# Softmax end in column halves, the last two chunks' logits by replicated weights, side products of the second MoE in batches, two more weight buffers

## The chip, the cores and the metric

One NeuronCore of a Trainium2 chip. Its engines run beside each other and meet by semaphores: PE (matrix products, into PSUM), PEld (the loading of the stationary operand for them), DVE (vector), ACT (activation functions, copies), POOL (general purpose) and SP, which here issues all the DMA transfers. The metric is the device time of one execution in microseconds (us); lower is better.

## The reference

Three layers follow each other on 1536 tokens of width 512:

```python
x = attention(q, k, v)              # clustered: a query sees the keys of its own cluster
h = x @ w_in                        # 1536 x 2048
g = (a0 + a1*h + a2*h*h + a3*h**3) / (1 + |b0|*|h| + |b1|*h*h + 1e-6)
x = g @ w_out                       # 1536 x 512, input of the second MoE
logits = x @ phi                    # 1536 x 32: 8 experts with 4 slots each
d = softmax(logits over the tokens) # axis 0
slot_input = (d.T @ x).reshape(8, 4, 512)
slot_out[e] = relu(slot_input[e] @ w1[e]) @ w2[e]     # 512 -> 1024 -> 512, 8 experts
c = softmax(logits over the slots)  # axis 1
out = c @ slot_out                  # 1536 x 512
```

## The kernel before, in words

The attention takes the first part of the span and isn't touched. What follows is written as if `w_out` came late: `logits` are made as `g @ (w_out @ phi)`, with `w_out @ phi` (the tile `wphi`) ready beforehand, and `d.T @ x` as `(d.T @ g) @ w_out`. So `g` is kept, `w_out` is applied to 32 slots and not to 1536 tokens, and the end of the kernel is a chain of small products.

*The unit loop.* The 1536 tokens are 3 blocks `t` of 512, the 2048 hidden columns 16 chunks `f` of 128; a unit n is one chunk of one block, 48 in all. `h_mm` makes h for a unit on PE (12 matrix products); `s1`, `s2`, `s3` make g from it on ACT, POOL and DVE (the last unit in two column halves); `s4`, four units later, turns g by four transposes (tile `gt`), copies it into the weight slots `gsl` on ACT, and every fourth unit adds four chunks to the logits: four products with 32 rows each (tile `l`), one in each quarter of the 128 rows, which run side by side. So row 32k+s of `l` holds slot s for the chunks of class k.

*The end of a block* (`block_end`): `e0` adds the four classes with the constant matrix `sum4` (tile `lsum`; every row then holds its slot's full logit, four times over) and takes the negative running maximum `nM` over the tokens; `e0b` turns the logits (`lt`) for the softmax over slots, and makes exp on ACT; `e2` turns exp (`dt`); `e3` makes `d.T @ g` (tile `dg`, 16 products of 512 columns in four quarters) and adds it to the running sum `U`. For blocks 0 and 1 this is spread over the next units. For block 2 it stands at the end, with nothing left to cover it.

*The chain behind it*: U is turned (`ut`, `uT`), multiplied by `w_out` (16 products, line 992), scaled by 1/sum (`sin`), turned and summed over the classes (line 999, `sT`), then by `w1` for experts 0 to 3 (line 1012, 32 products of 512 columns), relu, turned (line 1024) into the tile `HZ`; the same for experts 4 to 7; then the three softmaxes over slots are turned for the output (line 1036). Then `w2` (line 1083) in three column groups of 256, 128 and 128 columns, 64 products each; after each group `out_steps` sums the result over the row quarters (line 1047), splits it into a high and a low part (`SO4`, lines 1049 and 1051), multiplies by c (line 1058: six, three and three products) and copies the rows to the tile `ob`, from which SP writes 256 KB of output each (line 1069).

*Weights.* `w_out` (4 MB), `w1` (16 MB) and `w2` (16 MB) come as 36 loads of 1 MB in a fixed order (`queue`), the 16 of `w1` by halves of the contraction, 8 for experts 0 to 3 and then 8 for experts 4 to 7; those of `w2` are 8, 4 and 4 for the column groups. `freed` issues the next load when a buffer is given to it: one at every third unit while the list `waiting` has a buffer, then those freed at the end (the input's tiles, the unit loop's working tiles, the four `gsl` tiles after `dg`), then one for each weight tile that `used` says is read. There are 14 slots of 8 KB per partition (`NSLOT`): nine go to weights at first, five hold g. SP issues in program order, and a load that waits for its buffer holds up the ones behind it.

*Order.* PE's and SP's order is the program's; in the unit loop ACT's, DVE's and POOL's is set by a scheduler. `warm` puts in products whose result nobody reads.

Of the kernel before, what the change touches and what calls it, by code (L numbers as in the profile page):

```python
# [58 lines left out]
def tile_kernel(ctx, tc, qT, kT, v, cenT, cenP, consts, constsb, ab, w_in, w_out, phi, w1, w2, out, dbg=None):  # L59
# [665 lines left out]
    U = keep.tile([128, 512], F32, name="U")  # L725
    wphi = keep.tile([128, NF, NS], F32, name="wphi")
    POOL.tensor_scalar(wphi, wphi0, 1.0, 1.0, ALU.mult, ALU.mult)
    rctx.close()
    NSLOT = 14
# [99 lines left out]

    def s4(n):  # L830
# [3 lines left out]
        if k == 0:  # L834
            gsl[t, j] = sl_tile(F32, f"g{t}{j}")
        ps = psT.tile([128, 512], F32, tag="t", name="gt")
        for i in range(4):
            PE.transpose(ps[:, i * 128:(i + 1) * 128], g[:, i * 128:(i + 1) * 128], ident)  # L838
        ACT.copy(gsl[t, j][:, :, k * 128:(k + 1) * 128], ps.rearrange("p (i f) -> p i f", i=4))
        if k == 3:  # L840
            if j == 0:
                lps[t] = psL.tile([128, 512], F32, tag="l", name="l")
            for kk in range(4):
                PE.matmul(lps[t][32 * kk:32 * kk + 32, :], wphi[:, 4 * j + kk, :], gts.pop(n - 3 + kk),  # L844
                          start=(j == 0), stop=(j == 3))
            if j == 3:
                Ls[t] = keep.tile([128, 512], F32, tag="L", name="L")
                DVE.tensor_copy(Ls[t], lps.pop(t))


    def block_end(t):
# [13 lines left out]
        def e0b():  # L865
# [5 lines left out]
            if t == NB - 1:  # L871
                hold["dT"] = a_tile("dT")
# [25 lines left out]
        def e3():  # L898
# [11 lines left out]
            if t == NB - 1:  # L910
                freed(sl_tile, 4)

        return [e0, e0b, e2, e3, e1]

    def warm(k):

        for _ in range(k):
            ps = psH.tile([128, 512], F32, tag="h", name="warm")
            PE.matmul(ps[:, 0:256], ident, cst[:, 0:256], start=True, stop=True)
# [8 lines left out]
    for n in range(nunit + LAG):  # L928
# [6 lines left out]
        if 0 <= n - LAG:  # L935
            s4(n - LAG)
            if (n - LAG) % NF == NF - 1:
# [12 lines left out]
    manual = tc.manual_schedule(engines={mybir.EngineType.PE})  # L950
# [4 lines left out]
    sl2_p = ctx.enter_context(tc.tile_pool(name="sl2", bufs=4, reuse_waits="tile"))  # L955
    a_p = ctx.enter_context(tc.tile_pool(name="ap", bufs=3, reuse_waits="tile"))
    d_p = ctx.enter_context(tc.tile_pool(name="dp", bufs=1, reuse_waits="tile"))

    def sl2_tile(dt, name):
        return sl2_p.tile([128, 4, 512], dt, tag="sl2", name=name)  # L960
# [5 lines left out]
    for e in ends:  # L966
        e()
        warm(1)
    ps = psT.tile([128, 512], F32, tag="t", name="ut")
    for k in range(4):  # L970
        PE.transpose(ps[:, k * 128:(k + 1) * 128], U[:, k * 128:(k + 1) * 128], ident)
# [188 lines left out]
```

## Time and profile before

| | us |
|---|---|
| three runs | 548.85, 548.89, 549.78 |
| median | 548.89 |
| the profiled execution, its own time | 547.26 |
| its span, first to last instruction | 545.5 |
| PE busy in the span | 524.1 |

The span is cut by the profile into instructions of each engine. A row of the timeline or the chain gives a start, a duration and what ran; "issue" is time in which nothing that the profile shows was waited for.

### The profile page before, as it was taken

How to read it: one execution, taken by the hardware profiler on the slowest of the kernel's cores; microseconds unless marked ns; L12 is line 12 of the kernel's file. 1: busy time of each engine (PE TensorE's matmuls, PEld its weight loads, DVE VectorE, ACT ScalarE, POOL GpSimd, SP SyncE). 2: the span in 40 equal slices, each digit the busy share in tenths (PEclk: the TensorE clock that was granted, in tenths of full speed). 3: DMA queues.
4: the chain of work that ended last, by engine and by line, in shares of the span. 5: the costliest groups of instructions: out<-in, count | busy, mean ns of one | idle time of the engine just before them, and what ended most of it. 6: DMA issues, size and time to landing. Idle time of an engine off the chain costs nothing.

```text
span 545.5 us, 10069 instructions
## 1 busy us (share of the span) xinstructions
PE 524.1 (96%) x3518; PEld 342.3 (63%) x3521; DVE 414.0 (76%) x801; ACT 381.0 (70%) x693; POOL 274.5 (50%) x314
## 2 busy tenths in 40 slices
PE   8989999999999999999999999999999999988994
PEld 3555666566566666665666777777777767743463
DVE  6678889888798897988652799999799988941143
ACT  2777888869788788797874788878587868820111
POOL 3435767467655786567523655555455535601000
PEclk9999999999999999999999999999999999999999
DMA  8959869597767886667331566866567656479997
GB/s 231 281 141 255 240 206 268 185 256 192 247 192 233 252 247 191 211 198 195 126 101 59 192 245 225 295 225 227 189 225 273 239 176 224 170 318 369 419 420 282
DMA packets 43282, 125.71 MB, mean 230 GB/s; under 512 B 6432, under 2 KB 7328, under 8 KB 38624
## 3 DMA queue, kind: packets, MB, share of 16 engines
q1 hardware_dynamic: 43232, 125.07, 70.3%
q8 instruction: 28, 0.46, 0.4%
q14 instruction: 22, 0.18, 0.1%
HBM read 89.66 MB, written 15.73 MB: 193 GB/s over the span
## 4 chain that ended last, share of the span: by engine, by line
PE 75%; DVE 11%; ACT 5%; DMA 4%; issue 3%; SPq 1%; POOL 1%; DVEq 0%; POOLq 0%; ACTq 0%
PE av L414 10%; PE sT L401 9%; PE h L777 9%; PE h L780 8%; PE h L778 8%; PE s L377 5%; PE s L378 4%; DVE e L386 4%; PE gt L838 4%; PE pb L1083 3%; PE pb L1012 3%; PE l L844 2%; PE dg L902 2%; PE mf L230 1%; ACT e L390 1%
## 5 line engine op out<-in xcount | busy, mean ns | idle before, releaser
L386 DVE TENSOR_SCALAR_CACHE_REDUCE e<-s 128x768 f32<-128x768 f32 x96 | 91.6, 955 | 38.4 <-PE s L378 31.0
L390 ACT ACTIVATE e<-e,nv 128x768 f32<-128x768 f32 x96 | 89.9, 936 | 41.9 <-DVE e L386 35.2
L401 PEld LDWEIGHTS sT<-cst,e 128*128 128x128 f32 x576 | 61.4, 140 | 51.7 <-ACT eT L407 17.4
L401 PE MATMUL sT<-cst,e 128*128 128x128 f32 x576 | 83.7, 281 | 1.1 <-ACT eT L407 0.9
L407 ACT COPY eT<-sT 128x768 f32<-128x768 f32 x96 | 75.8, 789 | 9.3 <-PE sT L401 8.2
L414 PE MATMUL av<-eT,vt 128*64 128x384 f32 x384 | 82.0, 510 | 0.0
L777 PE MATMUL h<-xh,w 128*128 128x512 f32 x192 | 80.6, 420 | 0.0
L377 PE MATMUL s<-k,q 128*128 128x384 f32 x192 | 73.2, 381 | 4.3 <-DVE e L386 3.1
L544 POOL TENSOR_TENSOR w<-mh,ex 128x516 f32<-128x516 f32 x32 | 42.1, 1315 | 70.1 <-DVE ex L539 35.7
L778 PE MATMUL h<-xl,w 128*128 128x512 f32 x192 | 75.9, 395 | 0.0
L808 POOL TENSOR_SCALAR q<-u,babs 128x512 f32<-128x512 f32 x47 | 36.4, 775 | 73.6 <-ACT u L806 73.6
L378 PE MATMUL s<-k,q 80*128 80x384 f32 x192 | 64.8, 338 | 0.0
L810 POOL TENSOR_TENSOR q<-q,u 128x512 f32<-128x512 f32 x47 | 61.0, 1298 | 3.8
L780 PE MATMUL h<-xh,w 128*128 128x512 f32 x192 | 52.8, 396 | 0.0
L806 ACT ACTIVATE u<-h 128x512 f32<-128x512 f32 x47 | 28.0, 595 | 28.1 <-PE h L780 25.1
L777 PEld LDWEIGHTS h<-xh,w 128*128 128x128 f32 x192 | 36.2, 189 | 16.0 <-DVE r L826 3.4
L809 DVE TENSOR_TENSOR p<-p,h 128x512 f32<-128x512 f32 x47 | 32.1, 683 | 14.7 <-ACT p L807 14.5
L780 PEld LDWEIGHTS h<-xh,w 128*128 128x128 f32 x192 | 36.3, 189 | 8.9
L377 PEld LDWEIGHTS s<-k,q 128*128 128x128 f32 x192 | 36.4, 190 | 7.6 <-DVE e L386 5.0
L778 PEld LDWEIGHTS h<-xl,w 128*128 128x128 f32 x192 | 36.2, 189 | 7.2 <-issue 0.5
L817 ACT ACTIVATE r<-q,epsc 128x512 f32<-128x512 f32 (+1 forms) x49 | 33.8, 690 | 8.2 <-POOL q L810 6.8
L825 DVE SCALAR_TENSOR_TENSOR p<-p,ncoef,r 128x512 f32<-128x512 f32 (+1 forms) x49 | 35.9, 732 | 2.5 <-ACT r L818 1.6
(179 smaller groups left out, 999.4 us busy)
## 6 DMA issues: line engine op xcount, KB each, us to landing
wt<-w SPq DMA_DIRECT2D x32, 1024.0 KB, 8.0
w<-w_in SPq DMA_DIRECT2D x96, 256.0 KB, 3.1
raw<-w_in SPq DMA_DIRECT2D x16, 512.0 KB, 5.1
raw<-w_out SPq DMA_DIRECT2D x16, 512.0 KB, 4.3
w_in<-w SPq DMA_DIRECT2D x16, 512.0 KB, 3.7
k<-ka SPq DMA_DIRECT2D x32, 192.0 KB, 3.8
q<-qh SPq DMA_DIRECT2D x28, 192.0 KB, 5.1
w_out<-w SPq DMA_DIRECT2D x16, 256.0 KB, 3.8
```

The source lines that it names most:

```text
L377: PE.matmul(ps[:, c, 0:HS], o["q1"][:, it], o["k1"][:, w], start=True, stop=False)
L378: PE.matmul(ps[:, c, 0:HS], o["q2"][0:80, it], o["k2"][0:80, w], start=False, stop=True)
L386: DVE.tensor_scalar(e, s1s.pop(u)[:, :, 0:HS], -1.0, None, ALU.mult, ALU.min, accum_out=nvs[g][:, rest:rest + 1])
L390: ACT.activation(es[u], es[u], AF.Exp, scale=-1.0, bias=nvs[g][:, rest:rest + 1], accum_out=sums[g][:, rest:rest + 1])
L401: PE.transpose(ps[:, j // 3, j % 3 * 128:(j % 3 + 1) * 128], e[:, j, :], ident)
L407: ACT.copy(dst, eTp.pop(u)[:, :, 0:HS].rearrange("p c (j t) -> p c j t", j=3))
L414: PE.matmul(av[g][64 * h:64 * h + 64, 0:HS], vs[g // 2][:, h, j, :], eTs[g][:, h, j, :], start=(j == 0), stop=(j == 5))
L544: POOL.tensor_tensor(w.rearrange("p (r n) -> p r n", r=3), hold["mh"].bitcast(F32), hold["ex"].bitcast(F32), ALU.mult)
L777: PE.matmul(h, wh[:, c, :], xh[t][:, c, :], start=(c == 0), stop=False)
L778: PE.matmul(h, wh[:, c, :], xl[t][:, c, :], start=False, stop=False)
L780: PE.matmul(h, wl[:, c, :], xh[t][:, c, :], start=False, stop=(c == NCC - 1))
L810: POOL.tensor_tensor(q, q, u, ALU.mult)
```

## The change

Five edits, all from unit 45 on:

1. The logits of chunks 14 and 15 of the last block (units 46 and 47) no longer go through `l`. `wrep` holds the two chunks of `wphi` four times side by side (one POOL instruction), so a product with all 128 rows adds a chunk to the finished logits `lz` straight away, in two column halves; `sum4` is applied to the earlier chunks before (line 837), after their copy to `L`, which is now on ACT and not DVE. `gt` of the last unit is copied on DVE, behind the maximum.
2. The end of block 2 is written out in column halves (256 of 512): maximum, exp, turn, `dg`, `U`, turn of U, product with `w_out`, `sin`, `sT`. Halves of one step stand between halves of another on PE.
3. The first half of experts 4 to 7's `w1` product stands between experts 0 to 3's product and its turn; the turn for experts 4 to 7 stands behind `w2` of experts 0 and 1, the turns of c (12) behind expert 4. The parts of `out_steps` are taken in batches: the sum after expert 1 of the next group, three rows after expert 4, three after expert 6. The high/low split of slot outputs takes one DVE instruction on 64 rows where it took two on 32; that of c two on 32 where it took one on 64. The rows of a group go to ACT first, then DVE, by turns.
4. `NSLOT` is 16. The sum `sT` and the turned c lie in tiles that are free by then.
5. `warm`: 4 products in place of 15.

```diff
-    mxs = keep.tile([128, 8], F32, name="mxs")
+    mxs = keep.tile([128, 14], F32, name="mxs")
...
-    NSLOT = 14
+    NSLOT = 16
...
+    HALF = (slice(0, 256), slice(256, 512))
+    def logits_end(n):
+        if n == nunit - 2:
+            lps["all"] = [psH.tile([128, 512], F32, tag="h", name="lz")[:, 0:256] for _ in HALF]
+            for z, w in zip(lps["all"], HALF):
+                PE.matmul(z, sum4, Ls[NB - 1][:, w], start=True, stop=False)
+        for z, w in zip(lps["all"], HALF):
+            PE.matmul(z, wrep[n - nunit + 2], gts[n][:, w], start=False, stop=(n == nunit - 1))
...
+        if n >= nunit - 2:
+            logits_end(n)
         ps = psT.tile([128, 512], F32, tag="t", name="gt")
         for i in range(4):
             PE.transpose(ps[:, i * 128:(i + 1) * 128], g[:, i * 128:(i + 1) * 128], ident)
-        ACT.copy(gsl[t, j][:, :, k * 128:(k + 1) * 128], ps.rearrange("p (i f) -> p i f", i=4))
-        if k == 3:
+        if n == nunit - 1:
+            lps["gt"] = ps
+        else:
+            ACT.copy(gsl[t, j][:, :, k * 128:(k + 1) * 128], ps.rearrange("p (i f) -> p i f", i=4))
+        early = n == nunit - 3
+        if early or k == 3 and n < nunit - 1:
             if j == 0:
                 lps[t] = psL.tile([128, 512], F32, tag="l", name="l")
-            for kk in range(4):
-                PE.matmul(lps[t][32 * kk:32 * kk + 32, :], wphi[:, 4 * j + kk, :], gts.pop(n - 3 + kk),
-                          start=(j == 0), stop=(j == 3))
+            for kk in range(2 if early else 4):
+                PE.matmul(lps[t][32 * kk:32 * kk + 32, :], wphi[:, 4 * j + kk, :], gts.pop(n - k + kk),
+                          start=(j == 0), stop=(j == 3 or (t, j) == (NB - 1, 2) and kk > 1))
             if j == 3:
                 Ls[t] = keep.tile([128, 512], F32, tag="L", name="L")
-                DVE.tensor_copy(Ls[t], lps.pop(t))
+                if early:
+                    ACT.copy(Ls[t], lps.pop(t))
+                else:
+                    DVE.tensor_copy(Ls[t], lps.pop(t))
...
-            if t == NB - 1:
-                freed(sl_tile, 4)
...
+        if n == nunit:
+            wr = g_p.tile([128, 512], F32, tag="g", name="wrep", bufs=8)
+            POOL.tensor_scalar(wr[:, 0:256].rearrange("p (f r s) -> p f r s", f=2, r=4),
+                               wphi[:, NF - 2:NF, :].unsqueeze(2).to_broadcast([128, 2, 4, NS]), 1.0, 1.0, ALU.mult, ALU.mult)
+            wrep.extend(wr[:, i * 128:(i + 1) * 128] for i in range(2))
+            warms.append(psH.tile([128, 512], F32, tag="h", name="warm"))
         if n >= nunit:
-            warm((1, 3, 4, 1)[n - nunit])
+            warm((1, 2, 1, 0)[n - nunit])
...
+    for i, w in enumerate(HALF):
+        DVE.tensor_scalar(dT[:, w], lz[i], -1.0, None, ALU.mult, ALU.min, accum_out=nMh[i])
+    DVE.scalar_tensor_tensor(nM, nMh[0], nM0, nMh[1], ALU.min, ALU.min)
+    DVE.tensor_copy(gsl[T2, 3][:, :, 384:512], lps.pop("gt").rearrange("p (i f) -> p i f", i=4))
+    eT = a_tile("eT")
+    for i, w in enumerate(HALF):
+        ACT.activation(eT[:, w], dT[:, w], AF.Exp, scale=-1.0, bias=nM, accum_out=sb[i])
+    ACT.activation(corr, nM0, AF.Exp, scale=-1.0, bias=nM)
+    lt = psT.tile([128, 512], F32, tag="t", name="lt")
+    for i in range(4):
+        PE.transpose(lt[:, i * 128:(i + 1) * 128], dT[:, i * 128:(i + 1) * 128], ident)
+    d = a_tile("d").rearrange("p (i s) -> p i s", i=4)
+    for h in range(2):
+        ps = psR.tile([128, 512], F32, tag="r", name="dt")
+        for i in range(2):
+            PE.transpose(ps[:, i * 128:(i + 1) * 128], eT[:, (2 * h + i) * 128:(2 * h + i + 1) * 128], ident)
+        DVE.tensor_copy(d[:, 2 * h:2 * h + 2, 0:32], ps[:, 0:256].rearrange("p (i s) -> p i s", i=2)[:, :, 0:32])
...
+    pd = [psH.tile([128, 512], F32, tag="h", name="dg") for h in range(2)]
+    def dg(h, i):
+        for j in range(4):
+            PE.matmul(pd[h][32 * j:32 * j + 32, 0:256], d[:, i, 0:32], gsl[T2, j][:, i, HALF[h]],
+                      start=(i == 0), stop=(i == 3))
+    def new_U(h):
+        DVE.scalar_tensor_tensor(U[:, HALF[h]], U[:, HALF[h]], corr, pd[h][:, 0:256], ALU.mult, ALU.add)
+    def turn_U(h):
+        ps = psT.tile([128, 512], F32, tag="t", name="ut")
+        for k in range(2):
+            PE.transpose(ps[:, k * 128:(k + 1) * 128], U[:, (2 * h + k) * 128:(2 * h + k + 1) * 128], ident)
+        ACT.copy(uT[:, 2 * h:2 * h + 2, :], ps[:, 0:256].rearrange("p (k s) -> p k s", k=2))
+    for i in range(4):
+        dg(0, i)
+    new_U(0)
+    dg(1, 0)
+    dg(1, 1)
+    turn_U(0)
+    dg(1, 2)
+    dg(1, 3)
+    freed(sl_tile, 4)
+    new_U(1)
+    ce_second()
...
+    pw = [psR.tile([128, 512], F32, tag="r", name="pw") for h in range(2)]
+    def wo(kh, c):
+        for jj in range(2):
+            for k in range(2 * kh, 2 * kh + 2):
+                for j in range(2 * jj, 2 * jj + 2):
+                    q = 32 * (2 * (k % 2) + j % 2)
+                    PE.matmul(pw[c][q:q + 32, 0:256], uT[:, k, 32 * j:32 * j + 32],
+                              W["wo", j][0][:, k * 512 + 256 * c:k * 512 + 256 * c + 256],
+                              start=(kh == 0 and jj == 0), stop=(kh == 1 and jj == 1))
+    wo(0, 0)
+    turn_U(1)
+    wo(0, 1)
+    wo(1, 0)
+    wo(1, 1)
+    for j in range(1, 4):
+        used(("wo", j))
...
+    DVE.tensor_scalar(sin[:, HALF[0]], pw[0][:, 0:256], rS, None, ALU.mult)
+    ACT.activation(sin[:, HALF[1]], pw[1][:, 0:256], AF.Copy, scale=rS)
+    sT = U[:, 0:128].rearrange("p (c s) -> p c s", c=4)
+    def turn_in(h):
+        ps = psT.tile([128, 512], F32, tag="t", name="st")
+        for c in range(2):
+            PE.matmul(ps[:, c * 32:(c + 1) * 32], sin[:, (2 * h + c) * 128:(2 * h + c + 1) * 128], sum4[:, 0:32],
+                      start=True, stop=True)
+        DVE.tensor_copy(sT[:, 2 * h:2 * h + 2, :], ps[:, 0:64].rearrange("p (c s) -> p c s", c=2))
...
+    for c in range(NCC):
+        in_mm(0, c)
+    relu(0)
+    in_mm(1, 0)
+    in_mm(1, 1)
+    turn_h(0, 0)
+    turn_h(0, 1)
+    in_mm(1, 2)
+    in_mm(1, 3)
+    relu(1)
...
+            if c0 == 0 and e == 1:
+                turn_h(1, 0)
+                turn_h(1, 1)
+                crs = [turn_c(t) for t in range(NB)]
+            if c0 == 0 and e == 4:
+                for t in range(NB):
+                    split_c(t, crs[t])
+            for _ in range({1: 1, 4: 3, 6: 3}.get(e, 0)):
+                if outs:
+                    outs.pop(0)()
```

On PE, at the end of the logits (names: `gt` the turned g, `l`/`lz` the logits, `lt`/`dt` the turned logits and exp; x4 is four instructions), before:

```order
-L919 MATMUL warm<-cst 128x256 x4
-L838 MATMUL gt<-cst,p 128x128 x4
-L844 MATMUL l<-p,wphi 32x512 x4
-L919 MATMUL warm<-cst 128x256
-L860 MATMUL lsum<-L,cst 128x512
-L919 MATMUL warm<-cst 128x256
-L870 MATMUL lt<-cst,L 128x128 x4
-L919 MATMUL warm<-cst 128x256
-L894 MATMUL dt<-cst,dT 128x128 x4
```

and in the change:

```order
+L861 MATMUL l<-p,wphi 32x512 x2
+L935 MATMUL warm<-cst 128x256 x2
+L837 MATMUL lz<-L,cst 128x256 x2
+L839 MATMUL lz<-p,wrep 128x256 x2
+L851 MATMUL gt<-cst,p 128x128 x4
+L935 MATMUL warm<-cst 128x256
+L839 MATMUL lz<-p,wrep 128x256 x2
+L851 MATMUL gt<-cst,p 128x128 x4
+L1005 MATMUL lt<-cst,L 128x128 x4
+L1010 MATMUL dt<-cst,eT 128x128 x4
```

The sum over the classes (860, now 837) has moved ahead of the last two chunks, and the last chunk's product (839) stands ahead of its own turn. On ACT the copy to `L` has come in between the two halves of unit 47's division (817 is its logarithm, 818 the exponential):

```order
+L855 COPY g_5681<-gt 128x4x128
 L818 ACTIVATE r<-r 128x256
+L866 COPY L<-l 128x512
 L817 ACTIVATE r<-q,epsc 128x256
 L818 ACTIVATE r<-r 128x256
```

Further on PE, from the last `dg` products to the first of `w2` (`pw` the product with `w_out`, `ut` the turned U, `st` the turned `sin`, `pf` the products with `w1`, `ht` the turned relu):

```order
+L1071 MATMUL pw<-wt,uT 32x256 x8
+L1048 MATMUL ut<-cst,U 128x128 x2
+L1071 MATMUL pw<-wt,uT 32x256 x24
+L1090 MATMUL st<-cst,sin 128x32 x4
+L1123 MATMUL pf<-wt,U 32x512 x48
+L1141 MATMUL ht<-cst,h_5960 128x128 x4
+L1141 MATMUL ht<-cst,h_5962 128x128 x4
+L1123 MATMUL pf<-wt,U 32x512 x16
+L1208 MATMUL pb<-wt,HZ 32x256 x16
+L1141 MATMUL pb<-cst,h_6008 128x128 x4
+L1141 MATMUL pb<-cst,h_6010 128x128 x4
+L1208 MATMUL pb<-wt,HZ 32x256 x24
```

Each turn of a relu (1141) now has products of others between it and the product that feeds the relu, where before it stood right behind it. On SP, behind the last loads of the unit loop's own weights (`w`), with what each waits for:

```order
+L620 DMA w<-w_in_146 128x512 [waits DMAHW2_49,PE_49]
+L757 DMA wt<-w 128x2048
+L757 DMA wt<-w 128x2048 [waits DMAHW1_49,Activation_49]
 L757 DMA wt<-w 128x2048 [waits PE_49]
+L757 DMA wt<-w 128x2048 [waits DMAHW3_49,PE_49]
+L757 DMA wt<-w 128x2048 [waits DMAHW6_49,DMAHW7_49,DMAHW5_49,DMAHW4_49]
```

The first two loads of this piece are new here: the row with `PE_49` alone (the input's tile, after its last read) came right behind `w` before.

## Rows read from the trace of the kernel before

**Rows 1.** Page, part 2: granted clock of TensorE in tenths, 40 slices.

```profile
PEclk9999999999999999999999999999999999999999
```

**Rows 2.** Chain that ended last, 478 to 500 us: start, us, what.

```profile
478.44 0.48 DVE p L825
...
480.60 0.44 DVE p L827
...
488.02 3.64 PE dg L902 x32
...
494.05 3.69 PE pb L992 x32
...
497.76 0.76 DVE sin L996
...
498.56 1.09 PE pb L999 x8
...
499.68 0.30 DVE sT L1001
```

**Rows 3.** The same chain, 500 us to the end.

```profile
500.03 7.20 PE pb L1012 x64
...
507.90 0.66 PE pb L1024 x4
508.55 7.05 PE pb L1012 x64
...
516.34 0.66 PE pb L1024 x4
...
533.21 0.43 PE pb L1047 x2
...
534.73 0.93 PE pb L1058 x3
535.66 1.93 PE pb L1083 x64
...
539.11 0.31 DVE SO L1051
...
540.05 0.69 DVE ob L1068
```

**Rows 4.** Timeline of SP, 440 us to the end: start, us, line, transfers.

```profile
455.24 10.29 SPq L620 DMA_DIRECT2D w<-w_in  x6
471.67 44.07 SPq L757 DMA_DIRECT2D wt<-w  x22
```

**Rows 5.** Line 757, the load issued at 491.7 us: issue; time to landing.

```profile
L757 SPq DMA_DIRECT2D wt<-w x1: 328/328/328, 491.7 to 491.7; - x1
...
DMA to landing us min/median/max: 4.8/4.8/4.8
```

**Rows 6.** Line 757, the last load: issue; time to landing.

```profile
L757 SPq DMA_DIRECT2D wt<-w x1: 327/327/327, 515.4 to 515.4; - x1
...
DMA to landing us min/median/max: 19.9/19.9/19.9
```

**Rows 7.** Windows: stretch, us, busy of PE, PEld, DVE, ACT, POOL; clock, DMA share, GB/s.

```profile
492.00:535.00 43.00, 40.67 (x537) 21.24 (x536) 10.76 (x25) 5.61 (x10) 1.81 (x1) 1.00 1.00 405
540.00:545.00 5.00, 0.48 (x3) 0.04 (x1) 1.29 (x2) 0.59 (x1) 0.00 (x0) 0.80 0.60 225
```

**Rows 8.** Timeline, 473 to 486 us: start, us, engine, line, operation, tiles, shapes.

```profile
473.10 1.10 POOL L799 TENSOR_SCALAR q<-u,babs 128x256 f32<-128x256 f32 x2 [0.60 <-ACT u L798]
...
477.01 0.42 ACT L818 ACTIVATE r<-r 128x256 f32<-128x256 f32 x1
...
478.35 1.89 PE L919 MATMUL warm<-cst 128*128 128x256 f32 x8
478.55 0.59 ACT L839 COPY g<-gt 128x512 f32<-128x512 f32 x1
...
485.28 0.16 DVE L863 TENSOR_TENSOR mxs<-mxs 128x1 f32<-128x1 f32 x1
```

More of the change, by code (lines that the diff above doesn't have):

```diff
@@ L965, in tile_kernel @@
     freed(sl2_tile, 4)
[L966 to L971, printed above, removed]
-    uT = a_tile("uT").rearrange("p (k s) -> p k s", k=4)
-    DVE.tensor_copy(uT, ps.rearrange("p (k s) -> p k s", k=4))
-    warm(1)
-    manual.__exit__(None, None, None)
+    T2 = NB - 1
+    lz, dT = lps.pop("all"), Ls.pop(T2)
+    nM0, nM, corr = mxs[:, 1:2], mxs[:, 0:1], mxs[:, 3:4]
@@ new lines, in tile_kernel, with turn_c, split_c @@
+    cTs = []
+    def turn_c(t):
+        cr = a_tile("cr").rearrange("p (i r s) -> p i r s", i=4, r=4)
+        DVE.tensor_copy(cr, ce[t].unsqueeze(2).to_broadcast([128, 4, 4, 32]))
+        return cr
+    def split_c(t, cr):
+        ps = bank()
+        for i in range(4):
+            PE.transpose(ps[:, i * 128:(i + 1) * 128], cr[:, i].rearrange("p r s -> p (r s)"), ident)
+        tag = ("wphi", "U", "L")[t]
+        cTs.append(keep.tile([128, 512], F32R, tag=tag, name=f"cT{t}"))
+        ACT.copy(cTs[t], ps)
+        for q in (slice(32, 64), slice(96, 128)):
+            DVE.tensor_tensor(cTs[t][q, :], ps[q, :], cTs[t][q, :].bitcast(F32), ALU.subtract)
@@ new lines, in tile_kernel, with in_mm @@
+    turn_in(0)
+    turn_in(1)
+    HZ = sl_tile(F32, "HZ").rearrange("p a b -> p (a b)").rearrange("p (a k n) -> p a k n", a=2, k=8)
+    POOL.memset(HZ, 0.0)
+    pfs = {}
+    def in_mm(a, c):
+        for fh in range(2):
+            for e4 in range(4):
+                wt = W["w1", 4 * a + e4, c // 2][0]
+                o = (c % 2) * 1024 + fh * 512
+                PE.matmul(pfs[a][fh][32 * e4:32 * e4 + 32, :], sT[:, c, :], wt[:, o:o + 512],
+                          start=(c == 0), stop=(c == NCC - 1))
+        if c % 2 == 1:
+            for e4 in range(4):
+                used(("w1", 4 * a + e4, c // 2))
@@ new lines, in tile_kernel, with relu, turn_h @@
+    pfs[0] = [psH.tile([128, 512], F32, tag="h", name="pf") for _ in range(2)]
+    pfs[1] = [psT.tile([128, 512], F32, tag="t", name="pf") for _ in range(2)]
+    H1s = {}
+    def relu(a):
+        for kh in range(2):
+            H1 = H1s[a, kh] = a_tile("h1")
+            ACT.activation(H1, pfs[a][kh], AF.Relu)
+    def turn_h(a, kh):
+        ps, H1 = bank() if a else psR.tile([128, 512], F32, tag="r", name="ht"), H1s[a, kh]
+        for k in range(4):
+            PE.transpose(ps[:, k * 128:(k + 1) * 128], H1[:, k * 128:(k + 1) * 128], ident)
+        src = bass.AP(ps.tensor, ps.offset + 16 * a, [list(ps.ap[0]), [128, 4], [36, 4], [1, 4]])
+        hz = HZ[:, a, 4 * kh:4 * kh + 4, :]
+        dst = bass.AP(hz.tensor, hz.offset + 16 * a, [list(hz.ap[0]), [128, 4], [36, 4], [1, 4]])
+        DVE.tensor_copy(dst, src)
@@ L1094, in tile_kernel @@
         st()
+    manual.__exit__(None, None, None)
 def lay_out(inputs):
```

104 lines of the change are left out of this document (34 added, 70 removed).

## The prediction

> **What bounds the kernel now.** I read the page first: the clock stands at its full level in all 40 slices [rows 1]. Then the chain of what ended last, backwards from the end, because all edits bear on the end, behind the last `h` products: there the order, not the load, sets the time, so an average share of busy time says nothing. The reader is to see three stretches. From 478.44 to 500.03 us [rows 2] the chain goes from engine to engine: DVE finishes the last unit's g, PE makes the logits, DVE the maximum, ACT exp, PE `dg`, DVE `U`, PE the turn, DVE `uT`, PE the product with `w_out`, DVE `sin`, PE, DVE `sT`. Each step waits for the whole of the one before, and of these 21.6 us only the products at 488.02 (3.64) and 494.05 (3.69) are long work. From 500.03 to 537.59 [rows 3] PE works almost without a break, with three holes. From 537.59 to the end the last column group goes out.
>
> The second view is SP's timeline [rows 4] and the DMA share. From 492 to 535 us the DMA engines are 100% busy [rows 7], with the weights. Each load is 1 MB; 22 are issued from 471.67 on. The one issued at 491.7, right behind `dg`, lands 4.8 us later, at 496.5 [rows 5]; the last, 15 loads behind it, is issued at 515.4 and lands 19.9 us later, at 535.3 [rows 6]. That is 38.8 / 15 = 2.59 us a load. PE's last `w2` products start at 535.66 [rows 3], 0.3 us behind that landing. So **two chains end together**: PE's order, and the weight stream. A change that shortens one alone gives next to nothing; both have to be followed.
>
> **PE's order, part by part.** The sums are made against the profiled execution (547.26 us, of which the span is 545.5); the medians differ from it by 1.63, and I take the difference over to the median unchanged.
>
> *Logits (edit 1).* Before, the maximum is ready at 485.28 + 0.16 = 485.44 [rows 8], 4.4 us behind the last g (480.60 + 0.44 = 481.04 [rows 2]): four products, a copy, the sum over classes with 512 columns, a 512-column maximum. After, only the last chunk's product is left behind g: 256 columns for the second half. Four warm products of 256 columns take 1.89 [rows 8], so one takes 0.43 and its result some 0.17 more. Then the maximum of one half on DVE, which I put at 0.42 as other half-width operations, its reading 0.1, the merging 0.16 and gaps of 0.1: 1.4 us in all in place of 4.4. But ACT now makes the copy to `L` between the two halves of the division. A copy of this size takes 0.59, a half-width exponential 0.42 [rows 8], and consecutive ones overlap a little: 0.5 later for the second half, and DVE's first step waits for both (it begins at 478.44, when the second exponential ends [rows 2]). Bounds: nothing if the copy fits a gap, 1.0 if its wait for `l` adds to it; I take 0.5, near the row for the copy. Last g at 481.5, maximum at 482.95: **2.5 us earlier**. POOL's replication lies in front of a half that ACT takes up only 2 us later, at no cost; were that cover gone, it would cost 0.55, half of POOL's row of two such instructions, 1.10 [rows 8].
>
> *Exp to `dg`.* Before 488.02 - 485.44 = 2.6 us: exp of 512 columns, its sums, the turn, then a copy that waits behind another ACT instruction. After: two half exps (0.5 each), the turn of the second half (0.4), a copy of 64 columns per row on DVE, the first half of it hidden: 1.4 us, so `dg` starts at 484.35. **1.2 earlier**.
>
> *`dg` to the first `w1` product.* Before 500.03 - 488.02 = 12.0 us, of which PE's own work is about 3.4 + 3.4 (the two products without their last result's way out), 0.4 for the turn and 0.9 for `sin`. After, `U`, its turn and the copy of one half lie beside the other half's products: first half of `dg` 1.7, then half of the second covers the update of U (0.48, as the half-width operation of this kind at 478.44 [rows 2]), the other half covers the copy of `uT`. I find PE without a hole until the product with `w_out` ends: 3.4 + 0.4 + 3.4 = 7.2. Then the second half's scaling (0.6 with the way out) and its turn 0.5: 8.35, `w1` at 492.7. Bounds: if neither half's cover is enough, two handoffs of about 1.2 come back, 2.4 more; nothing speaks for less than PE's work. I stay at the value without holes since the covers (0.85 each) match the work they cover (0.48 and a copy, with some 0.3 for the way there and back), **3.65 earlier**. Up to here 7.35.
>
> *`w1`, `w2` (edit 3).* Work stays the same. Three holes go: 507.23 to 507.90 and 515.60 to 516.34, where the turn waits for relu, and 533.64 to 534.73, where the rows wait for the split of the slot outputs [rows 3]: 0.67 + 0.74 + 1.09 = **2.5**. In the new order each of these waits has at least 1.7 us of other products ahead of it. Bounds: 0 to 2.5 won. PE's last `w2` product would then end at 537.59 - 7.35 - 2.5 = 527.7.
>
> *Tail.* One split instruction of 0.31 [rows 3] falls away, and ACT's copies (0.59) go first and third where DVE's (0.69 [rows 3]) did: **0.4**.
>
> **The weight stream (edits 2 and 4).** Four buffers come free with the end of `dg`, now at 488.0 and not 491.67: 3.6 earlier. And two loads more have been issued by then, in the stretch behind the loop's own loads (455.24 + 10.29 = 465.5 to 471.67 [rows 4]) where SP only waits: the list of free buffers now has one for units 45 and 48. That is two loads fewer behind `dg`: 13 follow the first one, not 15. First landing 488.2 + 4.8, or, if the three before it are still under way, about 493.5; the last at 493.5 + 13 x 2.59 = 527.2, at 2.49 a load 525.9. The last two experts' products behind it take half of 1.93 [rows 3]: 527.0 to 528.4. Against PE's 527.7 I take **527.9** for the end of the last `w2` product: 9.7 us earlier than 537.59. With the tail 0.4 and nothing for the outputs, which queue behind the loads at either time, 10.1; I round to 10.0.
>
> **The warm products (edit 5).** Eleven of 15 go. The last matrix product before ends at 540.48, and the granted clock still falls from 1.00 to a mean of 0.80 in the window 540 to 545 [rows 7], that is to half, 1.2 GHz, for a part of it: the clock does fall here when PE stops. In the new order its longest hole is about 1.2 us (from the second `warm` to the end of the copy to `L`). I count nothing. The Trainium skill, page "TensorE: Matmul & The Clock Gate", Part 1, says that "the default state is throttled, and activity releases the throttle": by that rule the taking out of activity speaks against this edit. By it the result would be the second rival's; the trace shows the full clock throughout the chain of handoffs, with the warm products in it, and cannot show it without them.
>
> **Rivals.**
> - *The stream stays late* (two loads do not come earlier, or buffers in the unit loop's region hold SP up): 15 loads behind `dg` again, end of stream 532.4, PE's last product 533.4, gain 4.2 + 0.4: **544.3**. For it: SP's order lets one waiting load stop all. Against it: SP stands idle for 6 us before 471.67.
> - *The clock falls in the softmax end*, slower than before: PE's work from 478 to 492.7 is about 11 us at the full clock. At half it is 22; some 2 us of that takes up waits. If it lasts on through the first `w1` product (7.2 [rows 3]), another 7 come on top: 16 lost against 10 won, about **555**. It decides from about 12 us of PE work at the lower level on. Against it: PE's holes are short.
> - *Handoffs don't hide* (edit 2 brings half of its gain, the copy on ACT costs 1.0): 2.4 + 0.5 back, and one hole of edit 3 stays: **542.5**.
> - *It does nothing*: the last load still lands at 535.3; only the tail gains: **548.5**. Against it: that load waits for `dg` and for reads that all come earlier.
>
> **How the numbers follow.** My forecast (gain 8.5 to 11.5) gets 0.58, handoffs that don't hide (gain 5.5 to 8.5) 0.20, the late stream (3 to 5.5) 0.10, nothing 0.03, the clock 0.05 (0.04 of it slower), more than 11.5 gained 0.04. The predicted time is the likeliest's: 548.89 - 10.0 = 538.9. For 8 in 10 the range goes from 536.8 (both chains at their lower bounds: the stream at 525.9, no delay by the copy) to 543.2 (which takes in the handoffs and part of the late stream). Of 0.2% (1.1 us), about what a measurement can tell from no change: faster 0.93, same 0.03, slower 0.04.
>
> **What would show it.** The timeline after: maximum (997) done near 483.0; `dg` from 484.4; first `w1` product (1123) at 492.7 with no hole of PE over 0.3 us between the start of `dg` and the end of `pw`; SP's loads: two between 465 and 471, the four behind `dg` at 488; last load landing near 527; last `w2` product ending near 527.9 and PE waiting there for a load by less than 1 us; the granted clock 1.00 from 473 to 530. The prediction is wrong if PE's hole before the copy to `L` is longer than 1.5 us, if SP's load of the unit loop's region waits beyond 483, or if the clock falls.

## The result, and the profile after

The changed kernel takes **541.18 us** (median of 4 runs, 539.75 to 541.95) against 548.87 us for the kernel before beside it (median of 4): ratio 0.9861, 95% interval 0.9827 to 0.9895. That is 7.7 us less, where 10.0 were forecast (538.9, range 536.8 to 543.2).

The profiled execution took 541.77 us, its span 540.0. What comes ahead of the last `h` product is the same program in both kernels but for two weight loads that go out earlier, yet took 1.5 us more in this execution. So all positions below count **from the end of the last `h` product**: 472.57 us in the profile before, 474.12 in the one after. From there to the end of the span it is 72.90 before and 65.86 after: 7.04 won. Between kernels with the same program up to a point, these positions agree to 0.02 us, far better than times of whole runs do; they carry the readings below.

The chain of the changed kernel that ended last (start, us, what) answers to [rows 2, 3]:

```profile
473.19 0.95 PE h L780 x4
...
482.47 0.43 DVE p L827
...
485.99 2.73 PE dg L1039 x48
489.08 1.00 PE dg L1039 x16
...
491.31 2.80 PE pw L1071 x48
494.19 0.48 ACT sin L1084
...
495.34 10.44 PE pf L1123 x96
...
521.34 0.43 DVE SO L1197
521.82 0.70 PE pb L1172 x2
...
530.97 1.49 PE pb L1208 x48
```

The handoffs still alternate from 482.47 to 495.34, but the two `dg` and two `pw` rows now follow each other with only the turns between them. The maximum stands in DVE's timeline:

```profile
484.15 0.22 DVE L997 SCALAR_TENSOR_TENSOR mxs<-mxs 128x1 f32<-128x1 f32 x1
```

It ends at 484.37, 10.24 behind the last `h` product; before 12.87. Of the weight stream: SP's timeline (two of the 22 loads go out at 467.1 and 467.6, while SP stood waiting until 471.67 before [rows 4]), the last load with its time to landing, and the window that answers to [rows 7]:

```profile
467.12 42.09 SPq L757 DMA_DIRECT2D wt<-w  x22
```

```profile
L757 SPq DMA_DIRECT2D wt<-w x1: 328/328/328, 508.9 to 508.9; - x1
...
DMA to landing us min/median/max: 19.9/19.9/19.9
```

```profile
492.00:535.00 43.00, 40.77 (x606) 22.48 (x598) 12.72 (x30) 7.53 (x14) 1.81 (x1) 1.00 0.97 395
```

The last weight tile lands at 508.9 + 19.9 = 528.8, or 54.63 behind the last `h` product (62.79 before [rows 6]); PE's last `w2` products start at 530.97 in the chain, 2.2 us later, and not because of it. The stream no longer ends with PE's order: **PE's order alone is the bound now**. The clock is 1.00 from 492 to 535, as before [rows 7].

| step | forecast | measured |
|---|---|---|
| maximum | -2.5 | 12.87 to 10.24: -2.63 |
| maximum to `dg` | -1.2 | 2.58 to 1.55: -1.03 |
| `dg` to first `w1` product | -3.65 | 12.00 to 9.35: -2.65 |
| first `w1` to end of last `w2` product | -2.5 | 37.52 to 37.14: -0.38 |
| tail | -0.4 | 7.93 to 7.57: -0.36 |
| last weight landing | 527.2 | 528.8, less 1.55 of offset: 527.2 |

Two terms fell short: the third by 1.0, the fourth by 2.1. In the fourth stretch PE's timeline shows one idle time, and DVE's what it waits for:

```profile
517.25 3.67 PE L1208 MATMUL pb<-wt,HZ 128*32 128x256 f32 x80
521.82 0.70 PE L1172 MATMUL pb<-SO,cst 128*128 128x256 f32 x2 [0.90 <-DVE SO L1197]
```

```profile
517.10 4.21 DVE L1109 TENSOR_TENSOR cT<-pb,cT 32x512 fp32r<-32x512 f32 x6 [2.70 <-ACT cT L1107]
521.34 0.42 DVE L1197 COPY SO<-pb 128x256 f32<-128x256 f32 x1
```

The products of the first column block (48 of the 80 records) end at 520.04; their copy `SO` starts only at 521.34, since DVE is still at the split of c. Before, the split was three instructions of 64 rows:

```profile
520.05 1.91 DVE L1039 TENSOR_TENSOR cT<-pb,cT 64x512 fp32r<-64x512 f32 x3 [2.46 <-ACT cT L1038]
```

Six instructions of 32 rows take 4.21 us, three of 64 rows 1.91: the edit doubled the time. The third edit's text names it; the prediction gave it no price.

### The profile page after: what moved, and what is told of

Same layout as the page of the kernel before. It is cut to its first block, busy times and chain, and to the rows that moved or that the text cites. A ratio compares the mean times of both kernels' runs of the same rounds, so it can differ in the third digit from the quotient of the medians.

```text
span 540.0 us, 10173 instructions
## 1 busy us (share of the span) xinstructions
PE 519.7 (96%) x3569; PEld 341.8 (63%) x3569; DVE 415.8 (77%) x804; ACT 382.8 (71%) x699; POOL 274.9 (51%) x315
## 4 chain that ended last, share of the span: by engine, by line
PE 72%; DVE 13%; ACT 6%; DMA 4%; issue 2%; SPq 1%; POOL 1%; ACTq 0%; DVEq 0%
PE av L414 9%; PE sT L401 9%; PE h L777 8%; PE h L778 8%; PE h L780 8%; PE s L377 4%; PE s L378 4%; DVE e L386 4%; PE gt L851 3%; PE pf L1123 3%; PE pb L1208 2%; PE mf L230 2%; PE l L861 2%; ACT eT L407 2%; DMA raw<-w_in 2%
```

## The experiments

All are timed beside the kernel before on the same chip, in four groups (the kernel before took 547.58 to 548.87 beside them), so that rows are compared by ratios and positions. Positions are those of each run's one profile, from the end of the last `h` product.

| kernel | us median | ratio (95%) | last `w2` ends | last landing | span ends |
|---|---|---|---|---|---|
| before | 548.87 | | 64.97 | 62.79 | 72.90 |
| changed | 541.18 | 0.9861 (0.9827 to 0.9895) | 58.29 | 54.63 | 65.86 |
| 64-row split | 540.28 | 0.9849 (0.9824 to 0.9874) | 57.41 | 54.74 | 65.27 |
| early split | 540.16 | 0.9858 (0.9832 to 0.9884) | 57.42 | 54.72 | 64.98 |
| 14 buffers | 542.70 | 0.9900 (0.9877 to 0.9924) | 61.09 | 59.97 | 69.12 |
| before, 16 buffers | 548.06 | 0.9998 (0.9980 to 1.0016) | 64.42 | 57.69 | 72.34 |
| singles | 543.39 | 0.9924 (0.9903 to 0.9945) | 61.14 | 54.59 | 68.69 |
| turns direct | 540.65 | 0.9871 (0.9849 to 0.9894) | 59.19 | 55.52 | 66.77 |
| old logits | 542.74 | 0.9908 (0.9888 to 0.9929) | 61.00 | 57.37 | 68.56 |
| no interleave | 539.98 | 0.9863 (0.9839 to 0.9887) | 58.54 | 55.08 | 66.12 |
| 8 spread | 544.94 | 0.9943 (0.9920 to 0.9965) | 62.74 | 54.66 | 70.31 |
| 8 together | 542.96 | 0.9917 (0.9886 to 0.9948) | 60.41 | 56.30 | 67.98 |
| no warm | 541.07 | 0.9864 (0.9840 to 0.9888) | 58.62 | 55.08 | 66.19 |
| best | 539.69 | 0.9839 (0.9812 to 0.9866) | 57.25 | 54.61 | 64.82 |

**The split of c, in 64 rows.**

```diff
-        for q in (slice(32, 64), slice(96, 128)):
-            DVE.tensor_tensor(cTs[t][q, :], ps[q, :], cTs[t][q, :].bitcast(F32), ALU.subtract)
+        q = slice(64, 128)
+        DVE.tensor_tensor(cTs[t][q, :], ps[q, :], cTs[t][q, :].bitcast(F32), ALU.subtract)
...
-            r = slice(64, 128)
-            DVE.tensor_tensor(SO4[r, :], ps[r, :], SO4[r, :].bitcast(F32), ALU.subtract)
+            for r in (slice(32, 64), slice(96, 128)):
+                DVE.tensor_tensor(SO4[r, :], ps[r, :], SO4[r, :].bitcast(F32), ALU.subtract)
```

> One 64-row split of c instead of two of 32 rows (and two of 32 rows for SO4 instead of one of 64), all else as changed. In the profile of the changed kernel, 65.86 us pass from the end of the last h product to the end of the span, and 58.33 to the last w2 product. Theory (DVE's split of c, 6 x 0.69 us, delays the copy SO and PE waits 0.90 us for it): DVE then spends 3 x 0.69 = 2.1 us instead of 4.2, the hole ahead of the sum matmul is gone, and the last w2 product ends 0.9 us earlier, at 57.4; the end takes one more 32-row SO4 instruction, 0.2 to 0.3 us, so the span's end comes 0.6 to 0.7 us earlier. Rival (an instruction's time goes by its rows, so the split costs the same in one piece): the DVE row stays at 4.2 us in all and nothing moves. Rival (the weight stream ends the stage): the hole goes and the wait moves to the last weight tile; last w2 product within 0.2 us of 58.33.

DVE's timeline of this run:

```profile
516.55 1.91 DVE L1109 TENSOR_TENSOR cT<-pb,cT 64x512 fp32r<-64x512 f32 x3 [2.70 <-ACT cT L1107]
519.56 0.42 DVE L1197 COPY SO<-pb 128x256 f32<-128x256 f32 x1 [1.10 <-PE pb L1208]
...
521.49 0.86 DVE L1176 TENSOR_TENSOR SO<-pb,SO 32x256 fp32r<-32x256 f32 x2
```

The split is down to 1.91, `SO` starts 1.1 us after DVE became free, when its products end, and the last `w2` product ends 0.88 earlier, at the forecast 57.4. The end gains 0.59, the rest going to the extra split in the tail. Both rivals fall: the time does not go by rows, and the stream does not hold PE.

**The split of c, one expert earlier.**

```diff
-            if c0 == 0 and e == 4:
+            if c0 == 0 and e == 3:
```

> The three splits of c one expert earlier (behind expert 3 of the first column block instead of 4), all else as changed. Theory (DVE's split is late, not too much): DVE finishes it about 1.2 us earlier, ahead of the end of the block's last product, SO is copied on time, the 0.90 us hole ahead of the sum matmul is gone, and the last w2 product and the span's end come 0.9 us earlier than in the changed kernel (57.4 and 65.0 us after the last h product): ratio to the kernel before 0.984 instead of 0.986. Rival (the weight stream ends the stage): the gain is waited for at the last weight tile, end unchanged. Rival (the c copies aren't ready behind expert 3): a new hole of up to 1 us ahead of the c transposes, end unchanged.

PE's timeline now has no idle time at that place:

```profile
515.00 4.54 PE L1208 MATMUL pb<-wt,HZ 128*32 128x256 f32 x96
519.58 0.70 PE L1172 MATMUL pb<-SO,cst 128*128 128x256 f32 x2
```

The last `w2` product ends 0.87 earlier, the span 0.88. With the run before it, the 0.9 us is shown to be the place and length of DVE's split. (The ratio alone, with its interval, could not tell it.)

**14 buffers in the changed kernel; 16 in the kernel before.**

```diff
-    NSLOT = 16
+    NSLOT = 14
```

> 14 weight buffers instead of 16, all else as changed. Theory (with 14 the two last loads are issued behind the dg products, as in the kernel before, and the stream lands late): the last weight tile lands about 5 us later than in the changed kernel (54.63 us after the last h product), at 59 to 60, PE waits for it, and the last w2 product and the end come 1.5 to 3 us later. Rival (the stream has enough slack, buffers do nothing): last landing at or below 57, end within 0.3 us of the changed kernel.

> The kernel before, with 16 weight buffers instead of 14 (the small tile sT goes into the freed U to make room), and nothing else of the change. Theory (the kernel before is bound by PE's order behind the softmax end, the stream only by so much that its last landing of 62.79 us after the last h product comes within 2.3 us of the last w2 product): last landing some 5 to 8 us earlier, end 0 to 0.4 us earlier than before, ratio 0.999 to 1.000. Rival (the buffers carry the gain): most of the 7 us, ratio 0.988 or less.

PE's timeline with 14 buffers waits for transfers; these are two of three such waits (the third is 0.19):

```profile
528.73 0.65 PE L1208 MATMUL pb<-wt,HZ 128*32 128x128 f32 x16 [1.39 <-DMA wt<-w]
...
531.57 1.08 PE L1208 MATMUL pb<-wt,HZ 128*32 128x128 f32 x32 [0.73 <-DMA wt<-w]
```

The last tile lands 5.3 us later, the last `w2` product comes 2.8 later, the span ends 3.3 later: without edit 4 the stream is the bound, and 3.3 of the 7.0 are lost. The other 3.8 stay, though, since the stream moves with PE's order: `dg` ends earlier and frees its buffers earlier, so that the last landing comes at 59.97 even with 14 buffers, and at 62.79 before. The prediction's sentence that a change of one chain alone gives "next to nothing" does not hold here.

In the kernel before, the same two buffers bring the last landing 5.1 us forward, but the span only 0.56, and nothing that the ratio can tell (0.9998); 0 to 0.4 was expected. The 0.56 is not the stream's: PE lists no wait for a load behind its first `w1` product, with 14 buffers or with 16. Behind the turn of U the scheduler orders PE in that kernel, and with 16 buffers it put the three row products of the second column group behind 56 records of the third and not behind 22, so that they no longer wait 0.32 us for their split (the wait stands in the last profile lines of this text):

```profile
534.53 1.74 PE L1082 MATMUL pb<-wt,HZ 128*32 128x128 f32 x56
536.20 0.97 PE L1057 MATMUL pb<-cT,SO 128*128 128x512 f32 x3
```

So the **two chains that end together** [rows 3, 6] were a bound and one close behind it: before, the last tile landed 1.1 us ahead of the products that read it (62.79 against 63.92, the start of the last 32 records of `w2`). With PE's order several us shorter that slack is gone.

**Side products one by one; turns directly behind relu.**

```diff
-            for _ in range({1: 1, 4: 3, 6: 3}.get(e, 0)):
+            for _ in range(1 if e else 0):
```

> The side products of the w2 stage one behind each expert, as in the kernel before (sum matmul behind expert 1, one row product behind each later one), instead of sum, three rows, three rows; all else as changed. That makes 6 more breaks of the 32-row products by full-array ones (7 + 4 in place of 3 + 2). Theory (each break costs PE about 0.35 us: a gap of 0.31 from the last 256-column quarter product's start to the next full-array start where the products themselves follow at 0.053, and 0.20 where transposes follow at 0.11): 6 x 0.35 = 2.1 us plus a wait of up to 0.3 for the split of the slot outputs; last w2 product 1.8 to 2.6 us later than the changed kernel's 58.3 us after the last h product. Rival (breaks are free, only waits cost, as the prediction counted): 0 to 0.5 us later.

```diff
     relu(0)
+    turn_h(0, 0)
+    turn_h(0, 1)
     in_mm(1, 0)
     in_mm(1, 1)
-    turn_h(0, 0)
-    turn_h(0, 1)
...
+        if c0 == 0:
+            turn_h(1, 0)
+            turn_h(1, 1)
         so = bank()
...
-                turn_h(1, 0)
-                turn_h(1, 1)
```

> The turns of h1 directly behind their relu, as in the kernel before (ahead of the second half of w1, and ahead of the first w2 product), all else as changed. Theory (PE waits at each place for relu, as the kernel before did with 0.67 and 0.74 us; against that two breaks of about 0.35 us go, since the turns then stand between two stages): 1.4 lost, 0.7 won, last w2 product 0.5 to 1.0 us later than the changed kernel's 58.3 us after the last h product. Rival (holes alone count): 1.4 later. Rival (relu is hidden anyway): no change.

PE's timeline with singles, the first row product of the second block and what follows:

```profile
522.70 0.47 PE L1183 MATMUL pb<-cT,SO 128*128 128x512 f32 x1 [0.49 <-DVE SO L1176]
523.10 0.65 PE L1208 MATMUL pb<-wt,HZ 128*32 128x128 f32 x16
523.68 0.50 PE L1183 MATMUL pb<-cT,SO 128*128 128x512 f32 x1
```

It ends 2.85 later. A *break* is one change of PE from 32-row products to full-array ones and back. One wait of 0.49 for the split of `SO` is listed, and a gap of 0.14 stands at the same place of the third block; the other 2.2 is 6 breaks at 0.37. (The "as in the kernel before" of this expectation is true of the program's text only: there the program's order on PE ends with the turn of U, and behind it the scheduler had put five of six row products together, so this run does not undo edit 3. The changed kernel writes out the order of PE, ACT and DVE to the end. That is a sixth edit, which the list of five leaves out, and no run takes it by itself.) With the turns directly behind relu, 0.90 is lost, inside the range, by waits such as this one, twice (PE's timeline):

```profile
510.76 0.66 PE L1141 MATMUL pb<-cst,h 128*128 128x128 f32 x4
511.61 0.66 PE L1141 MATMUL pb<-cst,h 128*128 128x128 f32 x4 [0.19 <-ACT h L1136]
```

From 510.76 to the next product at 512.20 it is 1.44, where the changed kernel's eight transposes took 1.03: 0.41 a place, not the 0.7 that the expectation took over from the prediction. Its two saved breaks don't exist either (each place still has its one break); the two errors cancelled.

**The old logits; halves without interleave.**

```diff
+        if n == nunit - 1:
+            for kk in range(4):
+                PE.matmul(lps[t][32 * kk:32 * kk + 32, :], wphi[:, 4 * j + kk, :], gts.pop(n - k + kk),
+                          start=False, stop=True)
+            Ls[t] = keep.tile([128, 512], F32, tag="L", name="L")
+            DVE.tensor_copy(Ls[t], lps.pop(t))
+            logits_end(n)
...
-            PE.matmul(z, wrep[n - nunit + 2], gts[n][:, w], start=False, stop=(n == nunit - 1))
...
-        early = n == nunit - 3
+        early = False
```

> The last four chunks' logits as in the kernel before (four 32-row products behind the last chunk, the copy to L on DVE, then the sum matmul, in two column halves), all else as changed. Theory (the replicated weights take the copy and a handoff out of the path, 2.5 us by the prediction, 2.6 between the two profiles): the maximum comes 12.7 to 12.9 us after the last h product instead of 10.24, everything behind it as much later, end 2.4 to 2.7 us later. Rival (the path to the maximum is DVE's work on the last unit, logits hidden): under 0.5 us later.

DVE's timeline of this run (last `h` product at 472.19), then two windows (busy time of PE, PEld, DVE, ACT, POOL; clock, DMA share, GB/s):

```profile
481.77 0.69 DVE L850 COPY L<-l 128x512 f32<-128x512 f32 x1 [1.14 <-PE l L847]
...
484.75 0.22 DVE L1000 SCALAR_TENSOR_TENSOR mxs<-mxs 128x1 f32<-128x1 f32 x1
```

```profile
472.20:482.80 10.60, 7.31 (x41) 3.36 (x40) 8.69 (x18) 6.25 (x14) 2.85 (x5) 1.00 0.99 395
483.00:486.20 3.20, 3.20 (x14) 2.54 (x13) 1.78 (x6) 1.20 (x5) 0.00 (x0) 0.50 0.86 323
```

The maximum comes at 12.78, 2.54 later, and the span ends 2.70 later, so the rival (under 0.5) falls. But not all of it is the logits': here, after a stretch with PE busy 7.31 of 10.6 us, the granted clock went to half (1.2 GHz) for 3.4 us, from 482.92 on, while PE made the sum over the classes. These four records took 1.72 here and 1.13 in the changed kernel (PE's timelines, this run and then the changed kernel):

```profile
482.52 1.72 PE L837 MATMUL lz<-L,cst 128*128 128x256 f32 x4 [0.78 <-DVE L L850]
```

```profile
479.55 1.13 PE L837 MATMUL lz<-L,cst 128*128 128x256 f32 x4 [0.28 <-ACT L L866]
```

The second half's maximum step waits for them, so by an estimate from these rows some 0.6 of the 2.54 is the clock's, and another 0.17 behind it (maximum to `dg` 1.72, not 1.55). The replicated weights are then worth about 1.9 by themselves; the rest of the 2.63 between the two profiles would lie in the column halves of sum and maximum, which this run keeps. The clock fell in the profiled execution alone: its mean is 0.994 there and 0.997 to 0.998 in the five others, whose times vary too much (541.2 to 543.6) to settle the 0.6. The rule of the Trainium skill that the prediction weighed ("TensorE: Matmul & The Clock Gate", Part 1: the throttled state is the default) agrees with this profile; the changed kernel's shows nothing of it.

```diff
-    dg(1, 0)
-    dg(1, 1)
-    turn_U(0)
-    dg(1, 2)
-    dg(1, 3)
+    for i in range(4):
+        dg(1, i)
     freed(sl_tile, 4)
     new_U(1)
+    turn_U(0)
...
+    turn_U(1)
     wo(0, 0)
-    turn_U(1)
```

> The column halves stay, but without the interleave: all dg products of both halves, then the two turns of U, then all w_out products; all else as changed. From the first dg product to the first w1 product the changed kernel takes 9.35 us. Theory of the prediction (the interleave hides two handoffs of about 1.2 us each): 10.5 to 11.7. Theory of the breaks (two breaks go, 0.35 each, and the wait for the second half of U, at most 0.8, comes in): 9.1 to 9.6, end within 0.3 us of the changed kernel.

```profile
487.91 0.44 PE L1048 MATMUL ut<-cst,U 128*128 128x128 f32 x2 [0.31 <-DVE U L1043]
```

In PE's timeline above the second turn waits 0.31 for `U`. `dg` to `w1` takes 9.60 against 9.35. The prediction's two handoffs of 1.2 do not come back: the interleave brings 0.25 net, since it costs a break of its own (with the price below, its cover is worth some 0.6 by estimate). The other 2.4 of this stretch go with the halves and the written order, which no run takes apart. (The expectation counted two breaks less; by the order it is one.)

**The price of a break by itself.** Eight full-array products that nothing reads, added to the first half of `w1` (the output is unchanged; both kernels' edits in one block, with notes behind the #):

```diff
+    dm = psL.tile([128, 512], F32, tag="l", name="dm")
+
+    def dummy(k):
+        for _ in range(k):
+            PE.matmul(dm[:, 0:128], ident, cst[:, 0:128], start=True, stop=True)
...
     for c in range(NCC):
         in_mm(0, c)
+        dummy(1)                     # spread; four more in in_mm, behind fh == 0
+        dummy(8 if c == 1 else 0)    # together
```

> The changed kernel with 8 added full-array products (128x128, of constants, into a bank that nothing reads, no wait) in the first half of w1: one behind each run of 4 quarter products of 512 columns, so 8 breaks. Its pair has the same 8 in one place. Theory of the breaks (each change between 32-row and full-array products costs PE time by itself): this one ends 7 x 0.35 = 2.4 us later than its pair, up to 3.2 if a break behind 512 columns costs more (gap 0.52 to the next start where the products follow at 0.11). Rival (only waits for other engines cost): within 0.2 us of its pair.

> The changed kernel with 8 added full-array products (128x128, of constants, no wait) together behind the second chunk of the first half of w1, so one break. Theory of the breaks: 8 products of 0.1 to 0.2 us and one break, last w2 product 1.1 to 2.0 us later than the changed kernel's 58.3 us after the last h product. Rival (the added work is taken up by a wait further on): under 0.5 later.

PE's timeline, spread and then together:

```profile
494.06 1.06 PE L1123 MATMUL pf<-wt,U 128*32 128x512 f32 x8
495.05 0.49 PE L1153 MATMUL dm<-cst 128*128 128x128 f32 x2
495.47 1.07 PE L1123 MATMUL pf<-wt,U 128*32 128x512 f32 x8
496.47 0.49 PE L1153 MATMUL dm<-cst 128*128 128x128 f32 x2
```

```profile
499.19 3.64 PE L1123 MATMUL pf<-wt,U 128*32 128x512 f32 x32
502.76 2.05 PE L1151 MATMUL dm<-cst 128*128 128x128 f32 x16
504.75 2.78 PE L1123 MATMUL pf<-wt,U 128*32 128x512 f32 x24
```

With no wait recorded, the spread ones end the last `w2` product at 62.74, the others at 60.41: 2.33 for 7 breaks, **0.33 us a break**. That is the theory's number, shown without any other engine; what inside PE takes the time (the loads of the stationary operand change size as well) these runs do not separate. The second kernel lost 2.12, a little over its range. The Trainium skill, page "TensorEngine Tiling (Array Packing)", Key Properties, has a rule that bears on it: changing the tiling mode drains the array. These runs agree with it and give it a price; the prediction had not weighed it.

**No warm products.**

```diff
-            warm((1, 2, 1, 0)[n - nunit])
+            warm(0)
```

> The changed kernel without its 4 warm products between the last h product and the dg products; all else as changed. The prediction's step (the clock doesn't need them, they count nothing): granted clock 1.00 from the last h product to the last matrix product, dg start 11.8 us behind the last h product as in the changed kernel, end within 0.2 us. Rival (PE's waits in this stretch let the clock fall): the granted clock at half for some us between 0 and 12 us behind the last h product, dg start 0.2 to 1.7 us later; 4 to 7 us later if it stays down into the dg and w_out products.

The window from the last `h` product's end (473.0) to ahead of the `dg` products, then DVE's timeline:

```profile
473.00:483.60 10.60, 7.94 (x48) 4.77 (x46) 9.03 (x23) 6.66 (x15) 2.86 (x5) 1.00 1.00 391
```

```profile
481.32 0.42 DVE L996 TENSOR_SCALAR_CACHE_REDUCE L<-lz 128x256 f32<-128x256 f32 x1
...
481.68 0.42 DVE L827 SCALAR_TENSOR_TENSOR p<-r,p 128x256 f32<-128x256 f32 x1
482.88 0.42 DVE L996 TENSOR_SCALAR_CACHE_REDUCE L<-lz 128x256 f32<-128x256 f32 x1 [0.79 <-PE lz L839]
```

The clock holds at 1.00, so the warm products are not needed for it here, though PE is busy for only 7.94 of the 10.6 us (the mean clock is 0.996 to 0.997 in all six executions); yet `dg` comes 0.34 later, by a cause that neither theory named. DVE's list has changed: its first maximum step (996, 481.32) now stands ahead of the last unit's final step (827, 481.68), which in the changed kernel comes first (482.47, then 996). DVE's order in the unit loop is the scheduler's, not written out, and it moved when PE's work did, the run's only edit.

**A better version.** The early split, and the six row products of the second block together:

```diff
-            if c0 == 0 and e == 4:
+            if c0 == 0 and e == 3:
...
-            for _ in range({1: 1, 4: 3, 6: 3}.get(e, 0)):
+            for _ in range({1: 1, 4: 6}.get(e, 0)):
```

> The changed kernel with the split of c behind expert 3 instead of 4, and the six row products of the second column block in one batch behind expert 4 instead of two of three (one break less). The run with the early split alone ended its last w2 product at 57.42 us behind the last h product and its span at 64.98. Theory (hole gone, one break of 0.35 less): 57.1 and 64.6. Rival (the six copies of the rows delay the next copy of SO, PE waits for it): 57.4 or later.

```profile
522.00 1.66 PE L1183 MATMUL pb<-cT,SO 128*128 128x512 f32 x6
```

The batch of six is in PE's timeline above; the last `w2` product ends at 57.25, the span at 64.82, 1.04 earlier than the changed kernel. The median is the lowest of all (539.69, ratio 0.9839); that it beats the changed kernel rests on the positions, as the intervals overlap. Of the 0.35 of one break, 0.17 came: the quarter products behind the next sum take 0.15 longer, with no wait recorded. Why stays open.

## Why the prediction was right, and where its sum was off

- **The number.** The time lies in the range, but the gain of 7.7 lies in the class to which the prediction gave 0.20 (5.5 to 8.5), not in its forecast's (8.5 to 11.5, 0.58): two of its terms fell 3.1 short.
- **What bounds the kernel** was right in the main: two chains, and both moved. The stream's term landed on its forecast (527.2; the products behind it would end at 526.9 to 528.2 by its own terms, not 527.0 to 528.4), and the 14-buffer run shows why it had to be there. But PE did not wait for a load before (1.1 us of slack), and does not now: the stream ends 2.2 us before PE's last run of `w2` products, since PE is late.
- **Logits, -2.5**: measured -2.63, and the parts of the sum hold: the last g comes 0.32 later (0.5 was taken for the copy on ACT), the maximum 1.47 behind it (1.4 forecast). Undone alone, edit 1 is worth 1.9 to 2.5, as the clock fell in that profile.
- **Maximum to `dg`, -1.2**: measured -1.03; its parts were not run apart.
- **`dg` to `w1`, -3.65: mis-sized.** It measured -2.65. The step that failed is "PE without a hole until the product with `w_out` ends: 3.4 + 0.4 + 3.4 = 7.2". There was no hole, but it took 8.05 (485.92 to 493.97): two breaks are worth 0.67 of the missing 0.85 by the price of 0.33. The other 0.15 of the 1.0 lies in the turn of `sin` (1.30 behind `pw`, 1.15 forecast; 7.2, 0.6 and 0.5 add up to 8.3, not the 8.35 of the sum).
- **`w1`, `w2`, -2.5: mis-sized.** It measured -0.38. First, the "three holes" were not holes. They were gaps in the chain, where it passes through ACT or DVE; PE's timeline of the kernel before has work in them:

```profile
507.03 0.66 PE L1024 MATMUL pb<-cst,h 128*128 128x128 f32 x4
507.90 0.66 PE L1024 MATMUL pb<-cst,h 128*128 128x128 f32 x4 [0.21 <-ACT h L1021]
...
515.49 0.66 PE L1024 MATMUL pb<-cst,h 128*128 128x128 f32 x4
516.34 0.66 PE L1024 MATMUL pb<-cst,h 128*128 128x128 f32 x4 [0.19 <-ACT h L1021]
...
533.56 0.85 PE L1083 MATMUL pb<-wt,HZ 128*32 128x128 f32 x22
534.73 0.93 PE L1058 MATMUL pb<-cT,SO 128*128 128x512 f32 x3 [0.32 <-DVE SO L1051]
```

  Idle there is 0.21, 0.19 and 0.32. Measured by what the same eight transposes take without a wait (1.03), the two turns lost 0.42 and 0.31; the third cost 0.54 in all, by the stretch from `w1` to the last `w2` product in the kernel before with 16 buffers, where it is gone (36.98 against 37.52). So about 1.25 was to be won, not 2.5. Second, the edit made a hole of its own (0.9, shown by two runs). Third, its new order has 8 breaks from `w1` to the last `w2` product, the scheduler's had 7. These add up to no gain at all; the 0.3 that was nevertheless won beyond them is not assigned.
- **The tail, -0.4, and the warm products, nothing**: right, with -0.36 for the tail, and for the clock (1.00 without any of them). Taking out all of them moves DVE's order, which the prediction did not look at.
- **The rivals.** The stream stayed late in none but the 14-buffer run, which gives by its positions what that rival had described (a wait for the last tiles). The clock did not fall in the changed kernel; with the old logits it fell in one execution of six, for 3.4 us, and not for the 12 us of work that the rival asked for. The third rival's time, 542.5, came closer than the forecast's (538.9), but not by its mechanism: the handoffs do hide.

## What to carry to other kernels

A gap between two rows of the chain is a handoff, not idle time of the engine that comes back: before it is counted as a gain, read that engine's own timeline in the gap. Price an instruction by its count and columns when a change halves its rows, and give each place where small side products interrupt a run of 32-row products a price of its own, so that batching is worth as much as hiding. When two chains end close together, try each edit alone in both kernels, and read what moved: the two buffers ended no wait for a load in one, and were worth 3.3 us in the other.

## What the runs showed of the hardware that was not expected

- DVE's time did not depend on the rows: 0.68 to 0.70 us for 32x512 as for 64x512, and 0.42 to 0.43 for 32x256 as for 64x256. Three of 64 rows in a row started 0.60 apart, overlapping a little, the 32-row ones 0.70 apart; why is not shown.
- A change from 32-row products to full-array ones and back cost PE 0.33 us with no wait on any engine (0.37 by the singles).
- The clock kept its upper level (2.4 GHz) without the warm products; with the old logits and the warm products it went to the lower for 3.4 us, in the one execution that was profiled.
